# Value products of an RWKV feed-forward as seven half-size products, with weight sums kept in DRAM

## The chip, the cores and the metric

The kernel runs on one core of a Trainium2 chip. A core has a matrix engine (TensorE, in profiles PE, with its weight loads as PEld), a vector engine (VectorE, DVE), an activation engine (ScalarE, ACT), GpSimd (POOL) and SyncE (SP), which here only issues transfers. The metric is device time of one execution in microseconds (us); lower is better.

## What is computed

A local-global attention over 8 batches of 8 heads, 512 local and 32 global positions, head size 64, whose output is the input of a feed-forward in the manner of RWKV. All is float32.

```python
s_ll = np.where(np.abs(pos[:, None] - pos[None, :]) <= 32, scale * q_l @ k_l.T, -1e9)
out_l = softmax([scale * q_l @ k_g.T, s_ll]) @ [v_g, v_l]     # window of 32 to each side, and the global keys
out_g = softmax(scale * q_g @ [k_g, k_l].T) @ [v_g, v_l]
x = concatenate([out_g, out_l])                                # 8 batches, 544 positions, 512 channels
xk = mu_k * x + (1 - mu_k) * x_prev                            # x_prev: the position before
xr = mu_r * x + (1 - mu_r) * x_prev
k = maximum(xk @ w_k, 0)                                       # w_k: 512 x 1024
v = (k * k) @ w_v                                              # w_v: 1024 x 512
out = sigmoid(xr @ w_r) * v                                    # w_r: 512 x 512
```

## The kernel before

**Feed-forward.** Channels lie on the 128 partitions, tokens on the free axis, 256 tokens (`TOK`) to a step: each batch of 512 local tokens is two objects `Tokens` (halves of the batch), and the 8 x 32 global tokens make a seventeenth, at the end. float32 products are made of parts that TensorE takes in one pass (`F32R`): each operand is split into a high part and the rest, and `products` (L381 to 385) issues three matmuls per 128-row chunk, high x high, high x rest, rest x high, all 128x128 by 128x256, into a half of a PSUM bank. The three weights come as 64-bit words; `decode` turns a chunk of 128 x 512 into its two parts with ScalarE, VectorE and GpSimd, paced by `next(decoding)` in the code of the first batch, and the parts stay in SBUF for the whole run.

For each `Tokens`, `mix` makes xk and xr in parts (VectorE L408 and L412, ScalarE L416, GpSimd L417); `keys_and_gate` makes 8 chunks of k in 4 steps of 24 matmuls, each followed by relu on ScalarE (L429), the square on GpSimd (L431) and on ScalarE as high part (L434) and the rest on VectorE (L435), and then the gate in 2 steps of 24 (copy to SBUF L449, sigmoid L451); `values` makes the product with w_v in 4 steps of 24 matmuls, multiplies by the gate (VectorE L463) and stores through SP's queue (L474).

**Attention.** Heads go in units of two, units in pairs, two pairs to a batch. `scores` (32 matmuls of 64x64 tiles, L241), eight masked reductions on VectorE (L246), eight exponentials on ScalarE (L251), the division on GpSimd (L260), `transposes` (L273) and their copies; `scores_global` (L298, reductions L299 and L303); `transposes_global` (L322, L323); `weighted` (matmuls L339 for the windows, L352 for the global queries, L364 for the global keys; copies L370, L372 and L375). Its results xT are the input of `mix` of the same batch.

**Buffers and order.** PSUM has 8 banks: 2 for the feed-forward (tag m), 4 for scores and the global results (tag s), 2 for transposes and `weighted` (tag t). The code emits attention of batch b + 1 and the feed-forward of batch b in turns (`together`), a step at a time; `feed_forward` puts `values` of one `Tokens` behind `mix` of the next. From this program a planner, which simulates the engines when the kernel is built, fixes the order on each engine: it takes the ready instruction that comes earliest in the code, and places the semaphore waits. At run time every engine, and SP's queue of transfers, works strictly in that order. Inputs q and k (L198) and v (L203) of a pair have two buffers each, so the next pair's loads wait until the present pair's matmuls have read theirs. The first batch's attention and keys run beside the decoding of the weights, in an order written out at L572 to L659; batch 7 has no attention beside its feed-forward.

## Time and profile before

| | |
|---|---|
| median of 3 runs | 714.57 us (713.87 to 714.68) |
| profiled execution | 713.56 us, of which 711.8 us span |
| mean granted TensorE clock | 0.978 of full speed |
| matmuls of the feed-forward (L383 to 385) | 4080, of which `values` 1632 |
| transfers | 66.73 MB, mean 94 GB/s |
| stages: first batch's attention, weights | 0 to some 70 us |
| two pairs of heads beside a batch's feed-forward | 79.9 us |
| feed-forward of the last batch and the global tokens alone | 611.5 us to the end |

In the profile's rows an L is a line of the kernel. A group row gives line, engine, operation, output and inputs, shapes and count, then busy time in us, mean ns of one, idle time of the engine before them and what ended it. A window row gives the stretch in us, its length, for each engine the busy time and the count of instructions (PE, PEld, DVE, ACT, POOL, or PE alone), then the granted TensorE clock, the share of the transfer engines' time and GB/s. A wait row gives total us, times, and the longest. A timeline row gives start, length, engine, line, operation and count. Rows of SPq are SP's queue: what a transfer waited for before it was issued.

### The profile page before, as it was taken

To read this page: it belongs to the slowest core of one execution; us is meant where nothing else is said; L and a number is where in the kernel's file an instruction comes from. 1 tells how busy PE (TensorE), PEld (TensorE's weight loads), DVE (VectorE), ACT (ScalarE), POOL (GpSimd) and SP (SyncE) were. 2 spreads that over 40 slices of the span, in tenths; PEclk is the share of its full clock that TensorE was granted. 3 is DMA by queue.
4 is the path that set the end of the run, shared out by engine and by line. 5 is a ranking of instruction groups with operands and counts; after the bars stand their busy time and mean duration, and the time that the engine had idled before them with its cause. 6 is when DMAs were issued, how large, how long until landed. Compare 5 with 4: busy or idle time off the path is not lost.

```text
span 711.8 us, 18514 instructions
## 1 busy us (share of the span) xinstructions
PE 684.2 (96%) x7616; PEld 645.3 (91%) x7616; DVE 360.0 (51%) x1134; ACT 394.8 (55%) x1075; POOL 298.6 (42%) x325
## 2 busy tenths in 40 slices
PE   5789799999999999999999999999999999999997
PEld 3568689989999999999999999899999999999997
DVE  5797976347254362736354363636354352534511
ACT  5877976365565565646565565646565553332420
POOL 6577685136253353424243353424243351323420
PEclk9788889999999999999999999999999999999999
DMA  8735334151423040403222040403222020000000
GB/s 343 279 98 205 128 124 167 39 179 38 158 74 107 16 164 31 164 32 96 98 84 97 17 163 31 164 30 107 88 90 91 16 80 26 17 16 30 2 30 30
DMA packets 21716, 66.73 MB, mean 94 GB/s; under 512 B 2176, under 2 KB 10880, under 8 KB 21632
## 3 DMA queue, kind: packets, MB, share of 16 engines
q1 hardware_dynamic: 21632, 65.55, 25.9%
q8 instruction: 60, 0.98, 0.6%
q14 instruction: 24, 0.20, 0.1%
HBM read 56.63 MB, written 8.91 MB: 92 GB/s over the span
## 4 chain that ended last, share of the span: by engine, by line
PE 77%; DVE 9%; ACT 7%; issue 3%; POOL 2%; DMA 2%; SPq 0%; POOLq 0%; DVEq 0%
PE ps_m L383 21%; PE ps_m L385 20%; PE ps_m L384 20%; PE ps_t L273 4%; PE ps_t L339 4%; PE ps_s L241 3%; ACT Pt L251 3%; DVE xfull L412 2%; PE ps_t L364 2%; DVE Pt L246 2%; POOL k L431 1%; DVE kkl L435 1%; DMA raw_qk<-qk 1%; PE ps_t L322 1%; PE ps_s L352 1%
## 5 line engine op out<-in xcount | busy, mean ns | idle before, releaser
L383 PE MATMUL ps_m<-xkh,wk_h 128*128 128x256 f32 x544 | 157.0, 290 | 2.5 <-ACT gate L446 2.5
L383 PE MATMUL ps_m<-kkh,wv_h 128*128 128x256 f32 x544 | 154.7, 284 | 0.0
L384 PE MATMUL ps_m<-xkl,wk_h 128*128 128x256 f32 x544 | 153.6, 283 | 0.0
L385 PE MATMUL ps_m<-xkh,wk_l 128*128 128x256 f32 x544 | 152.9, 281 | 0.0
L385 PE MATMUL ps_m<-kkh,wv_l 128*128 128x256 f32 x544 | 151.2, 278 | 0.3 <-POOL wv_l L182 0.3
L384 PE MATMUL ps_m<-kkl,wv_h 128*128 128x256 f32 x544 | 151.0, 278 | 0.0
L260 POOL TENSOR_TENSOR Pt<-Pt,ssum 128x512 f32<-128x512 f32 x64 | 67.8, 1060 | 156.0 <-DVE ssum L211 152.6
L251 ACT ACTIVATE Pt<-Pt,m 128x160 f32<-128x160 f32 x256 | 106.5, 417 | 40.6 <-DVE m L246 39.6
L431 POOL TENSOR_TENSOR k<-relu 128x512 f32<-128x512 f32 x68 | 73.4, 1079 | 125.8 <-ACT relu L429 125.8
L429 ACT ACTIVATE relu<-ps_m 128x512 f32<-128x512 f32 x68 | 40.6, 596 | 125.0 <-PE ps_m L385 122.8
L383 PEld LDWEIGHTS ps_m<-xkh,wk_h 128*128 128x128 f32 x544 | 104.0, 192 | 4.5 <-ACT gate L446 2.8
L383 PEld LDWEIGHTS ps_m<-kkh,wv_h 128*128 128x128 f32 x544 | 102.2, 188 | 3.6 <-issue 2.8
L384 PEld LDWEIGHTS ps_m<-xkl,wk_h 128*128 128x128 f32 x544 | 104.9, 193 | 0.0
L385 PEld LDWEIGHTS ps_m<-xkh,wk_l 128*128 128x128 f32 x544 | 104.0, 191 | 0.0
L385 PEld LDWEIGHTS ps_m<-kkh,wv_l 128*128 128x128 f32 x544 | 102.2, 188 | 0.5 <-POOL wv_l L182 0.5
L384 PEld LDWEIGHTS ps_m<-kkl,wv_h 128*128 128x128 f32 x544 | 102.2, 188 | 0.0
L435 DVE TENSOR_TENSOR kkl<-k,kkh 128x512 fp32r<-128x512 f32 x68 | 51.4, 756 | 98.0 <-POOL k L431 96.9
L246 DVE CUSTOM_DVE_ANT_0 Pt<-ps_s,masks 128x160 f32<-128x160 f32 x256 | 66.9, 318 | 45.7 <-PE ps_s L241 45.7
L383 PE MATMUL ps_m<-xrh,wr_h 128*128 128x256 f32 x272 | 79.6, 293 | 0.0
L384 PE MATMUL ps_m<-xrl,wr_h 128*128 128x256 f32 x272 | 76.9, 283 | 0.0
L385 PE MATMUL ps_m<-xrh,wr_l 128*128 128x256 f32 x272 | 76.8, 282 | 0.0
L417 POOL TENSOR_TENSOR xkl<-xfull,xkh 128x512 fp32r<-128x512 f32 x34 | 44.7, 1314 | 74.3 <-ACT xkh L416 74.3
(93 smaller groups left out, 1279.6 us busy)
## 6 DMA issues: line engine op xcount, KB each, us to landing
raw_qk<-qk SPq DMA_DIRECT2D x32, 768.0 KB, 5.7
raw_v<-v SPq DMA_DIRECT2D x32, 640.0 KB, 4.9
out_l<-gate SPq DMA_DIRECT2D x32, 256.0 KB, 2.2
w<-w_k SPq DMA_DIRECT2D x8, 512.0 KB, 9.3
w<-w_v SPq DMA_DIRECT2D x8, 512.0 KB, 3.6
w<-w_r SPq DMA_DIRECT2D x4, 512.0 KB, 3.9
out_g<-gate SPq DMA_DIRECT2D x2, 256.0 KB, 2.1
mu_k_sb<-mu_k SPq DMA_DIRECT2D x1, 2.0 KB, 11.2
```

The costliest lines, as they stand in the source:

```text
L246: nc.vector.tensor_tensor_reduce(out=Pt[:, i], in0=place(e, t, h), in1=masks[:, e, slots[t][1]], op0=ALU.add, op1=ALU.min, scale=-scale, s ...
L251: nc.scalar.activation(Pt[:, i], Pt[:, i], AF.Exp, bias=low_x[:, i:i + 1], scale=-1.0, accum_out=ssum[:, i:i + 1],)
L260: nc.gpsimd.tensor_mul(out, Pt[:, each, at:at + n], rinv.unsqueeze(2).to_broadcast([P, 4, n]))
L273: nc.tensor.transpose(tp[:, i], r.Pt[:, 4 * e + i, SG * e:SG * e + W], ident)
L339: nc.tensor.matmul(op[t][h * D:(h + 1) * D, j, e, a], s.v[:, h, i], r.PT[:, e, 2 * t + h, a * BL:(a + 1) * BL], start=(t, h) not in begun, ...
L383: nc.tensor.matmul(out, w_h[:, i, cols], x_h(i), start=(i == 0), stop=False)
L384: nc.tensor.matmul(out, w_h[:, i, cols], x_l(i), start=False, stop=False)
L385: nc.tensor.matmul(out, w_l[:, i, cols], x_h(i), start=False, stop=(i == n - 1))
L417: nc.gpsimd.tensor_sub(lo[:, both], xf, hi[:, both].bitcast(F32))
L429: nc.scalar.activation(rk, kp, AF.Relu)
L431: nc.gpsimd.tensor_mul(k2, rk, rk)
L435: nc.vector.tensor_sub(kl, k2, kh.bitcast(F32))
```

## The change

**Seven products.** For each batch the product of w_v (512 channels by 1024) with the squared keys (1024 by 512 tokens) is cut in halves in all three directions and made in Winograd's form of Strassen's scheme: seven products of half size on sums and differences, in place of eight. A1 and A2 index the halves of the weights, B of the keys, the second index of B the half of the batch. Sums of the weights, S1 = A21 + A22, S2 = S1 - A11, S3 = A11 - A21, S4 = A12 - S2, are made once; of the keys, T1 = B12 - B11, T2 = B22 - T1, T3 = B22 - B12, T4 = B21 - T2, in each batch. The products are A11 B11, A12 B21, S2 T2 (`values_1`) and S3 T3, S1 T1, A22 T4, S4 B22 (`values_2`), of 4 chunks x 2 x 3 = 24 matmuls each. Two banks X and Y take turns; sums of products stay in a bank or are made on VectorE and ScalarE through three SBUF tiles. The first product's tokens get their channels in two writes, at different times; the gate product is on GpSimd where its input is in SBUF.

**Keys.** The squares stay whole (`k2p`: B11, B21, B12, B22, T2, with T1, T3 and T4 written over B11, B12 and B21) and are split into parts only as operands: 14 tiles of 128x512 a batch, B blocks on ScalarE and VectorE, T blocks on ScalarE and GpSimd. Before it was 8 tiles a batch.

**Weights of the values.** `value_weights` decodes two chunks at a time, makes the sums, splits them, and writes A11 to S4 in parts to a DRAM scratch (8 writes of 1 MB). They are no longer in SBUF; `load_left` reads the left side of each product as two tiles of 512 KB, through 5 buffers, two products ahead, in every batch. Their pools take the place of the first stage's (`stage`, `first_units`, `sums`).

**Order.** `values_1` of the batch before goes ahead of the keys of half 0, `values_2` ahead of those of half 1; in the first batch both halves' keys come first, then both gates, then the products. The global tokens keep four products (`values_of_one`), with their keys between `values_1` and `values_2` of the last batch.

**Attention in one piece.** From batch 2 on the matmuls of a `scores` and of a `weighted` are chained (`Run`): each follows the one before on TensorE with raised priority, and the first has a wait on all the copies that the later ones need: `scores` on the last reads of its banks, `weighted` on the copies of the transposes and on the reduction L303 of the next pair's `scores_global` (`reads["g"]`).

```diff
-    stage = ctx.enter_context(tc.tile_pool(name="stage", bufs=3))
...
-    gatep = ctx.enter_context(tc.tile_pool(name="gatep", bufs=2))
+    gatep = ctx.enter_context(tc.tile_pool(name="gatep", bufs=3))
     tmpp = ctx.enter_context(tc.tile_pool(name="tmpp", bufs=3))
-    mlp1 = ctx.enter_context(tc.tile_pool(name="mlp1", bufs=1))
-    mlp = ctx.enter_context(tc.tile_pool(name="mlp", bufs=2))
+    sump = ctx.enter_context(tc.tile_pool(name="sump", bufs=3))
+    k2p = ctx.enter_context(tc.tile_pool(name="k2p", bufs=1))
+    dramp = ctx.enter_context(tc.tile_pool(name="dramp", bufs=1, space=bass.MemoryType.DRAM))
...
+    stage = place(early_s, "stage", 3, side="right")
+    first_units = place(early_u, "first_units", side="right")
...
+    def split(val, hi, lo, engine=None):
         nc.scalar.copy(hi, val)
-        nc.gpsimd.tensor_sub(lo, val, hi.bitcast(F32))
+        (engine or nc.gpsimd).tensor_sub(lo, val, hi.bitcast(F32))
...
+    LEFT = ("A11", "A21", "A12", "A22", "S1", "S2", "S3", "S4")
+    HC = NF // 2
+    scratch = dramp.tile([P, len(LEFT), HC, 2, TOK], F32, name="scratch")
+    def value_weights():
+        for i in range(HC):
+            A, S = (sums.tile([P, 4, 2, TOK], F32R, tag="x", name=f"left_{x}") for x in "as")
+            s = sums1.tile([P, 4, TOK], F32, tag="s", name="s")
+            a = []
+            for j in range(2):
+                val = decode(staged.pop(0), "s").rearrange("p (j n) -> p j n", j=2)
+                split(val, A[:, 2 * j:2 * j + 2, 0], A[:, 2 * j:2 * j + 2, 1])
+                a.append(val)
+            nc.vector.tensor_add(s[:, 0], a[0][:, 1], a[1][:, 1])
+            nc.vector.tensor_sub(s[:, 2], a[0][:, 0], a[0][:, 1])
+            nc.vector.tensor_sub(s[:, 1], s[:, 0], a[0][:, 0])
+            nc.vector.tensor_sub(s[:, 3], a[1][:, 0], s[:, 1])
+            split(s, S[:, :, 0], S[:, :, 1])
+            for j, part in ((0, A), (4, S)):
+                nc.sync.dma_start(out=scratch[:, j:j + 4, i], in_=part.bitcast(F32))
+            load_chunk()
+            load_chunk()
+            yield
+    V1 = (("A11", "B11"), ("A12", "B21"), ("S2", "T2"))
+    V2 = (("S3", "T3"), ("S1", "T1"), ("A22", "T4"), ("S4", "B22"))
+    to_load = [a for a, _ in V1 + V2] * B + ["A11", "A21", "A12", "A22"]
+    left = []
+    def load_left():
+        if to_load:
+            a = LEFT.index(to_load.pop(0))
+            for i in range(0, HC, 2):
+                part = leftp.tile([P, 2, 2, TOK], F32R, tag="a", name="a")
+                nc.sync.dma_start(out=part.bitcast(F32), in_=scratch[:, a, i:i + 2])
+                left.append(part)
...
+        run = Run(reads["s"] if slots[0][0].b > 1 else None)
...
+    class Run:
+        def __init__(self, copies=None):
+            self.copies, self.last = copies, None
+        def matmul(self, *a, **kw):
+            if self.copies is None:
+                nc.tensor.matmul(*a, **kw)
+                return
+            if self.last is not None:
+                with tc.issue_after(self.last.ins), tc.high_priority():
+                    self.last = nc.tensor.matmul(*a, **kw)
+                return
+            self.last = nc.tensor.matmul(*a, **kw)
+            for c in self.copies:
+                tc.add_manual_dep(
+                    self.last.ins, c.ins.name,
+                    mybir.DependencyInfo(mybir.DependencyClass.Sync, mybir.DependencyReason.DATA),
+                )
...
+        reads["g"] = nc.vector.tensor_tensor_reduce(
...
+    class Keys:
+        def __init__(self, tokens):
+            self.tokens = tokens
+            self.k, self.parts = {}, {}
+        def block(self, name):
+            self.k[name] = k2p.tile([P, HC, TOK], F32, tag=name, name=name)
+            return self.k[name]
+        def keys(self, t):
+            n = self.tokens.index(t) + 1
+            return t.keys([self.block(f"B{i}{n}") for i in (1, 2)])
+        def differences(self):
+            k = self.k
+            k["T1"], k["T3"], k["T4"] = k["B11"], k["B12"], k["B21"]
+            for out, a, b in (("T1", "B12", "B11"), ("T2", "B22", "T1"), ("T3", "B22", "B12"), ("T4", "B21", "T2")):
+                nc.vector.tensor_sub(k[out] if out != "T2" else self.block("T2"), k[a], k[b])
+        def split(self, *names):
+            for b in names:
+                self.parts[b] = []
+                for i in range(0, HC, 2):
+                    h, l = (rightp.tile([P, 2, TOK], F32R, tag=x, name=f"b{x}") for x in "hl")
+                    split(self.k[b][:, i:i + 2], h, l, nc.vector if b[0] == "B" else nc.gpsimd)
+                    self.parts[b].append((h, l))
+        def product(self, out, b, fresh=True):
+            right = self.parts.pop(b)
+            for i in range(HC):
+                a, (b_h, b_l) = left[i // 2], right[i // 2]
                 for j in range(2):
-                    products(vp[:, j], wv_h, wv_l, slice((e0 + j) * P, (e0 + j + 1) * P),
-                             lambda f: self.kk_h[f], lambda f: self.kk_l[f], NF)
-                    if j == 0:
-                        yield
-                o = self.gate[:, e0:e0 + 2]
-                nc.vector.tensor_mul(o, vp, o)
-                self.store(slice(e0, e0 + 2), o)
-                yield
-    FF_STEPS = 10
+                    a_h, a_l = (a[:, i % 2, x, j * P:(j + 1) * P] for x in range(2))
+                    for n, (w, x) in enumerate(((a_h, b_h), (a_h, b_l), (a_l, b_h))):
+                        nc.tensor.matmul(
+                            out[:, j], w, x[:, i % 2], start=fresh and (i, j, n) == (0, 0, 0),
+                            stop=(i, n) == (HC - 1, 2), skip_group_check=True,
+                        )
+            del left[:HC // 2]
+            load_left()
+        def bank(self):
+            return psum("m").rearrange("p (j n) -> p j n", j=2)
+        def sum(self):
+            return sump.tile([P, 2, TOK], F32, tag="sum", name="sum")
+        def values_1(self):
+            t = self.tokens[0]
+            X, Y = self.bank(), self.bank()
+            self.product(X, "B11")
+            c11, self.u2 = self.sum(), self.sum()
+            nc.scalar.copy(c11, X)
+            yield
+            self.product(Y, "B21")
+            nc.vector.tensor_add(c11, Y, c11)
+            t.write(0, c11)
+            yield
+            self.product(X, "T2", fresh=False)
+            nc.scalar.copy(self.u2, X)
+            yield
+            self.split("T3", "T1", "T4")
+        def values_2(self):
+            t0, t1 = self.tokens
+            u2, u3 = self.u2, self.sum()
+            X, Y = self.bank(), self.bank()
+            self.product(X, "T3")
+            nc.vector.tensor_add(X, X, u2)
+            nc.scalar.copy(u3, X)
+            self.split("B22")
+            yield
+            self.product(Y, "T1")
+            nc.vector.tensor_add(u3, Y, u3)
+            t1.write(1, u3)
+            yield
+            self.product(X, "T4", fresh=False)
+            t0.write(1, X)
+            yield
+            self.product(Y, "B22", fresh=False)
+            nc.vector.tensor_add(u2, Y, u2)
+            t1.write(0, u2)
+            yield
...
+        for n, t in enumerate(this.tokens):
             t.mix()
             if before is not None:
-                yield from before.values()
-            yield from t.keys_and_gate()
-            before = t
+                yield from (before.values_1, before.values_2)[n]()
+            if n:
+                this.split("B11", "B21")
+            yield from this.keys(t)
+            if n:
+                this.differences()
+                this.split("T2")
+            yield from t.gates()
...
+                weighted(pair, xTs, PG, copies=A.copies + C.copies + [copy, reads["g"]] if pair[0].b > 1 else None)
...
+        first[1].mix("k")
+        for _ in keys[1]:
             next(decoding)
             yield
-        first[1].mix()
-        for _ in keys[1]:
-            next(decoding, None)
-            yield
-        for t in first:
-            yield from t.values()
-    beside_heads(rest_of_first(), 2 * FF_STEPS - 2)
-    last = None
+        yield from first[0].gates(whole_gate=False)
+        first[1].mix("r")
+        yield from first[1].gates(whole_gate=False)
+        early_u.close()
+        early_s.close()
+        nonlocal leftp, rightp
+        leftp, rightp = place(ctx, "leftp", 5, side="right"), place(ctx, "rightp", 6, side="right")
+        load_left()
+        load_left()
+        last.split("B11", "B21")
+        last.differences()
+        last.split("T2")
+        yield from last.values_1()
+        yield from last.values_2()
...
+    def end():
+        yield from steps[0]
+        t.mix()
+        yield from before.values_1()
+        yield from final.keys(t)
+        yield from t.gates()
+        yield from before.values_2()
+        final.split("B11", "B21")
+        yield from final.values_of_one()
```

130 lines of the change are left out of this document (74 added, 56 removed).

## Prediction, made before the changed kernel was timed

> **What bounds the kernel now.** I read the page first (busy shares, slices, the chain by engine), then windows of TensorE, then the waits. From the page:
>
> ```profile
> span 711.8 us, 18514 instructions
> PE 684.2 (96%) x7616; PEld 645.3 (91%) x7616; DVE 360.0 (51%) x1134; ACT 394.8 (55%) x1075; POOL 298.6 (42%) x325
> ...
> PE   5789799999999999999999999999999999999997
> ...
> PEclk9788889999999999999999999999999999999999
> DMA  8735334151423040403222040403222020000000
> ...
> PE 77%; DVE 9%; ACT 7%; issue 3%; POOL 2%; DMA 2%; SPq 0%; POOLq 0%; DVEq 0%
> ```
>
> TensorE is the bound from the sixth slice (about 89 us) on, at a full granted clock; no other engine is near it. But busy PE only says that some matmul is under way (a line's mean of 280 ns is latency, not cost), so a saved matmul must be priced by its pace. Windows that hold known blocks of matmuls give that; their counts in brackets include neighbours that reach in, so I count from the code:
>
> ```profile
> 97.00:707.80 610.80, 606.54 (x6851) 582.74 (x6849) 282.68 (x900) 320.21 (x858) 233.50 (x241) 1.00 0.22 77
> 614.46:625.34 10.88, 10.88 (x98) 1.00 0.07 26
> 509.99:512.93 2.94, 2.94 (x29) 1.00 0.00 0
> 513.28:516.11 2.83, 2.83 (x28) 1.00 0.26 93
> ```
>
> The first row is everything from 97 us to the last matmul: TensorE stands for 4.26 us of 610.8. The second is `values` of one token half beside no attention: 96 matmuls in 10.88 us, 113.3 ns each, 2.72 us for a block of 24. The other two are single blocks of 24 between pieces of attention: 2.94 and 2.83 us. The extra 0.1 to 0.2 us is the change to and from attention's small matmuls.
>
> The waits of TensorE and two windows, the first a `weighted` of the middle batches, the second the last one:
>
> ```profile
> PE ps_s L241 <- DMA raw_qk<-qk: 6.3, 3, 5.1
> PE ps_t L339 <- DVE mg L303: 3.9, 10, 0.4
> ...
> 491.35:496.32 4.97, 4.58 (x121) 4.28 (x120) 4.97 (x11) 2.29 (x9) 3.08 (x4) 1.00 0.47 192
> 607.22:611.49 4.27, 4.27 (x121) 4.08 (x120) 3.20 (x8) 0.62 (x1) 1.40 (x1) 1.00 0.02 4
> ...
> 492.57 0.58 DVE L303 CUSTOM_DVE_ANT_0 Pg<-ps_t,low,mg 128x384 f32<-128x384 f32 x1
> ```
>
> Ten times `weighted` is cut and stands 0.4 us for VectorE's L303, which still reads the banks it needs; the uncut one takes 0.70 us less for the same matmuls.
>
> **The change part by part.**
>
> *Products.* Per batch, `values` had 2 halves x 4 x 8 x 3 = 192 matmuls; seven products of 4 x 2 x 3 = 24 are 168. The operand shapes stay. So 24 go in each of 8 batches; the global tokens keep their 96. At 113.3 ns that is 8 x 2.72 = **-21.8 us**; at 2.94 a block, -23.5. I take the lower, since the number of changes to attention barely falls. From 97 us on TensorE has no slack, so what is removed there shows in full if the operands are on time.
>
> *Engines behind the products, per batch.* The rows:
>
> ```profile
> L435 DVE TENSOR_TENSOR kkl<-k,kkh 128x512 fp32r<-128x512 f32 x68 | 51.4, 756 | 98.0 <-POOL k L431 96.9 <-PE ps_m L384 1.1
> L434 ACT ACTIVATE kkh<-relu 128x512 fp32r<-128x512 f32 x68 | 43.3, 636 | 1.6
> L463 DVE TENSOR_TENSOR gate<-ps_m,gate 128x512 f32<-128x512 f32 x34 | 23.5, 691 | 94.1 <-PE ps_m L385 94.1
> L417 POOL TENSOR_TENSOR xkl<-xfull,xkh 128x512 fp32r<-128x512 f32 x34 | 44.7, 1314 | 74.3 <-ACT xkh L416 74.3
> L260 POOL TENSOR_TENSOR Pt<-Pt,ssum 128x512 f32<-128x512 f32 x64 | 67.8, 1060 | 156.0 <-DVE ssum L211 152.6 <-PE ps_m L385 3.5
> ...
> 509.99:549.95 39.96, 39.57 (x466) 37.83 (x462) 19.10 (x67) 23.25 (x64) 15.51 (x17) 1.00 0.25 87
> 549.95:589.90 39.95, 39.56 (x445) 38.17 (x442) 19.18 (x66) 21.93 (x63) 16.04 (x17) 1.00 0.13 48
> ```
>
> The last two windows are one batch: 79.9 us with DVE 38.3, ACT 45.2, POOL 31.6. VectorE loses 8 kkl and 4 gate products (8.8 us) and gains 6 splits of B11, B21, B22, 4 differences of twice that width and 5 operations on the products: 6 x 0.756 + 8 x 0.756 + 5 x 0.691 = 14.0; it ends at 43.5. ScalarE loses 8 squares (5.1) and gains 14 casts and 3 copies of like size, 17 x 0.636 = 10.8: 50.9. POOL gains 8 splits of T blocks and 3 gate products, 8 x 1.314 + 3 x 1.060 = 13.7: 45.3. A batch now lasts about 77 us, so all three stay under 66%: hidden. If that cover failed, the price would be the chain behind a single product, about 1.5 us (0.691 plus 0.636 and the hops); it lies beside the next product's 2.72 us, since X and Y alternate. T2, the last operand to be made, has the gate blocks (5.8 us) and two products ahead of it. I put the leftover stalls, from a burst of score reductions ahead of such an operation, at **+2** for the run, between 0 and 12 (1.5 us in each of 8 batches).
>
> *Streamed left halves.* Each batch reads 7 x 1 MB, as 14 loads of 512 KB.
>
> ```profile
> raw_qk<-qk SPq DMA_DIRECT2D x32, 768.0 KB, 5.7
> ...
> w<-w_v SPq DMA_DIRECT2D x8, 512.0 KB, 3.6
> ...
> 114.46:117.00 2.54, 2.54 (x24) 2.54 (x23) 2.54 (x4) 0.73 (x3) 2.54 (x4) 1.00 1.01 419
> ...
> SPq L474 <- DVE gate L463: 210.5, 21, 28.2
> ...
> 488.38 0.83 SPq L198 DMA_DIRECT2D raw_qk<-qk  x2
> ...
> 508.81 1.25 PE ps_s L241 x32
> ```
>
> The 7.3 MB add 95 GB/s to the 48 to 87 of the batch windows; the queue moved 419 at full share. One product's 1.05 MB takes 2.5 us at that, a product 2.72: even back to back the stream keeps up, and two and a half products lie ready at the start of each burst. A half freed at a product's middle lands 3.6 us later, 4.96 us after that product began, and is needed at 2 x 2.72 + 1.36 = 6.8. Cost nothing, as long as SP issues each load when its buffer is free. The next pair's `raw_qk` loads have slack: issued at 488.4 behind the scores of one pair, they are read from 508.8 on and land in 5.7. Bound: one whole landing, 3.6 us, per burst (below, third rival).
>
> *Attention in one piece.* From batch 2 on the score and `weighted` matmuls follow each other, and the first waits for all the copies, for `weighted` also for L303 of the next pair (`reads["g"]`). By the last row above L303 ended at 493.2, 1.8 us after `weighted` began at 491.35. The planner must put other matmuls there, and the next gate block (2.9 us) is at hand. Best: 10 x 0.70 = -7.0. Worst: TensorE stands the whole 1.8 us, and everything behind it on its queue with it, so 10 x (1.8 - 0.7) = +11. I take **-4**, nearest the row of the uncut piece, with some cuts moved into a gate block. The score runs wait for the reductions of the scores before, several steps back: nothing.
>
> *Start.* The sums of the value weights, their way through DRAM and the new order fall into the stretch where TensorE isn't yet full:
>
> ```profile
> 60.00:80.00 20.00, 19.95 (x217) 17.46 (x215) 18.11 (x45) 16.80 (x41) 11.49 (x11) 1.00 0.51 174
> 80.00:97.00 17.00, 12.32 (x76) 10.88 (x74) 13.70 (x35) 14.95 (x38) 15.09 (x16) 0.70 0.27 83
> 97.00:115.80 18.80, 18.80 (x263) 17.35 (x262) 14.85 (x41) 15.93 (x42) 11.99 (x10) 1.00 0.58 186
> 115.80:149.00 33.20, 32.88 (x401) 31.17 (x401) 13.24 (x56) 13.99 (x49) 11.63 (x15) 1.00 0.27 99
> ...
> L182 POOL TENSOR_TENSOR wv_l<-w,wv_h 128x512 fp32r<-128x512 f32 x8 | 10.8, 1353 | 2.7 <-ACT wv_h L181 2.7
> ...
> L408 DVE TENSOR_TENSOR diff<-xT 128x256 f32<-128x256 f32 x64 | 32.3, 543 | 14.8 <-ACT xT L375 14.3
> ...
> 111.20 0.69 DVE L178 SCALAR_TENSOR_TENSOR w<-w,ps_s 128x512 int32<-128x512 int32 x1
> ...
> 115.78 0.28 PE L383 MATMUL ps_m<-kkh,wv_h 128*128 128x256 f32 x1
> ```
>
> Batch 0's `values` began at 115.8. In the 55.8 us before it DVE was busy 46.7, ACT 47.7, POOL 38.6. Added on VectorE: 16 sums and 4 doubled `diff` at 0.543 (10.9), T1 and T2 as four of 0.756 (3.0), B11 and B21 as four (3.0), less 8 kkl (6.0): +10.9, more than the 9.1 that were free. POOL: 8 half-size pieces of the sums' splits at 1.353 and two of T2 at 1.314: +13.4 against 17.2 free. And nothing may start until the last A11 and A12 have been split (1.35), written as 1 MB (about 5, from 3.6 for half of it) and read again (3.6): 10 us behind the last decode, which ended on VectorE at 111.9 (L178). That is 121.9, 6 us later. Of the window that follows, 33.2 less 21.8 of products = 11.4 us is attention, part of which can go ahead. I take **+4**, between -3 (the mix of half 1 is split, so its keys need less ahead of them; TensorE idled 4.7 us in 80 to 97) and +18 (the whole 10 us plus the overfull engines, nothing brought forward).
>
> Rows on one operation at two prices, same line, two instructions each:
>
> ```profile
> 488.87 0.88 DVE L412 SCALAR_TENSOR_TENSOR xfull<-diff,mu_k_sb,xT 128x256 f32<-128x256 f32 x2
> ...
> 490.92 1.64 DVE L412 SCALAR_TENSOR_TENSOR xfull<-diff,mu_r_sb,xT 128x256 f32<-128x256 f32 x2
> ```
>
> So VectorE operations nearly double at times. The Trainium skill, in "SBUF — State Buffer", section "Who interferes with whom", says why that may be: VectorE, with two inputs in SBUF, and GpSimd take turns on one pair of ports, and the later one waits for the whole instruction. By that rule the 13.4 us added on POOL at the start would come on top of VectorE's and push `values` back by up to as much; it is the mechanism of the first rival.
>
> **Sum.** 713.56 us is the profiled execution's time (1.8 us around its span of 711.8): -21.8 - 4 + 4 + 2 = 693.8. The median of the runs shown is 1.0 us higher: **694.8**.
>
> **The rivals.**
> *Start late, still faster.* VectorE and POOL, both overfull, hold each other up, and batch 0's products begin 20 us late with little to fill in: 14 us above the forecast, 709. For it: 60 to 80 us has VectorE at 18.1 of 20, and the doubled operation above. Against: attention can fill in, and wv's decode is now due ahead of the gates. 0.16.
> *Better than forecast.* Start at -3, pieces at -7, no stalls: 683. For it: the almost unbroken row from 97 us. 0.10.
> *Loads late, slower.* SP is one queue. A store waits there for its gate product, up to 28.2 us in the row above; a left load behind it isn't issued though its buffer is free, and each of two bursts a batch stands a whole landing: 16 x 3.6 = 58, so 752; half of them, 723. It decides from 25 / 16 = 1.6 us a burst on: then nothing is left. Against: SP's order follows the planned time of each wait, and its waits today cost TensorE almost nothing. 0.11, told as 735.
> *Waits in every batch.* `weighted` pays its +11 and products stall by the bound of 12: the gain is gone, about 714. 0.05.
>
> **How the numbers follow.** Forecast 0.58, its own range 686 to 702. Range 683 to 712: it takes in the forecast, the late start and half of the better case. A measurement of this kernel can tell about 0.2% (1.4 us) from no change. Faster: 0.58 + 0.16 + 0.10 = 0.84; the same 0.04; slower 0.12.
>
> **What would show it.** Right: two pairs of heads last 75.5 to 77.5 us instead of 79.9; TensorE's waits name no left tile; `values` of the last batch keep 2.7 us a product; the first product of batch 0 begins at 118 to 126. Wrong: TensorE waiting for a DMA into `a`, for L303 ahead of `weighted`, or for ScalarE's and VectorE's reads of X and Y; DVE and POOL full up to 130 us.

## The result and the profile after

| | before | after |
|---|---|---|
| median of the runs | 714.22 us (713.76 to 714.68, 4 runs) | 747.67 us (743.83 to 748.07, 4 runs) |
| ratio, with its 95% interval | | 1.0456 (1.0421 to 1.0492) |
| span of the profiled execution | 711.8 us | 746.2 us |
| first product of batch 0 begins at | 115.8 us | 137.8 us |

The changed kernel is 4.6% slower, where 694.8 us was forecast with a range of 683 to 712. TensorE does 192 matmuls less and its span is 34.4 us longer. The page of the changed kernel, with the lines that answer to those shown of the kernel before:

```profile
span 746.2 us, 18626 instructions
...
PE 684.0 (92%) x7424; PEld 639.5 (86%) x7424; DVE 429.3 (58%) x1178; ACT 427.9 (57%) x1151; POOL 428.7 (57%) x417
...
PE   5788985889999999899989999899989999898996
...
PEclk9779998799999999999999999999999999999999
DMA  9636589695215456363826184536536181452546
...
PE 64%; DVE 13%; ACT 5%; issue 2%; DMA 2%; POOL 1%; POOLq 0%; ACTq 0%; DVEq 0%; SPq 0%
```

TensorE's busy time is what it was (684.0 against 684.2 us) although it has less to do, and from the sixth slice on its line of slices has 8s and one 5 (112 to 131 us) among the 9s, where it had 9s alone. On the chain that ended last VectorE rose from 9% to 13%. So the loss has two sides: TensorE stands more, and its matmuls take longer. The windows of TensorE up to the first product show the first place (columns as in the windows of before; the last pair of numbers is DMA share and GB/s):

```profile
80.00:97.00 17.00, 15.38 (x145) 14.43 (x143) 13.41 (x31) 10.23 (x26) 15.22 (x12) 1.00 0.72 233
97.00:115.80 18.80, 18.00 (x184) 15.66 (x184) 15.60 (x33) 15.60 (x30) 14.13 (x12) 0.91 0.80 288
115.80:137.80 22.00, 12.66 (x143) 9.73 (x141) 13.84 (x66) 18.71 (x60) 10.91 (x11) 0.77 0.85 292
```

In the last 22 us, in which the kernel before was already at its products, TensorE is busy 12.66, at a granted clock of 0.77. The waits of TensorE name the second place (what waited, what released it: us in total, times, longest):

```profile
PE ps_m L575 <- DVE gate L527: 15.0, 6, 3.1
...
PE ps_t L353 <- ACT xT L457: 6.0, 2, 5.6
PE ps_m L575 <- ACT sum L610: 3.0, 2, 2.9
PE ps_m L575 <- ACT sum L593: 2.0, 1, 2.0
...
PE ps_m L575 <- DMA a<-scratch: 2.0, 3, 1.6
```

L575 is the matmul of a product, L527 the copy of a gate block out of PSUM: six times a product waits for it. The transposes of the global scores (L402) of the same pair in two batches that follow each other, and the window from the one to the other, give the length of a batch:

```profile
417.87 0.60 PE L402 MATMUL ps_t<-ident,Pg 128*128 128x128 f32 x4
...
497.28 0.49 PE L402 MATMUL ps_t<-ident,Pg 128*128 128x128 f32 x3
```

```profile
417.87:497.28 79.41, 76.50 (x901) 73.00 (x899) 43.85 (x135) 49.62 (x137) 46.24 (x46) 1.00 0.52 180
```

79.4 us against 79.9 before and some 77 forecast, with VectorE, ScalarE and POOL busy for 43.9, 49.6 and 46.2 us (forecast: 43.5, 50.9 and 45.3). The sums of the engines' work were right; that it would be hidden was not.

### The profile page after: what moved, and what is told of

Its sections match the earlier page's. It is cut to its first block, busy times and chain, and to the rows that moved or that the text cites. A ratio compares the mean times of both kernels' runs of the same rounds, so it can differ in the third digit from the quotient of the medians.

```text
span 746.2 us, 18626 instructions
## 1 busy us (share of the span) xinstructions
PE 684.0 (92%) x7424; PEld 639.5 (86%) x7424; DVE 429.3 (58%) x1178; ACT 427.9 (57%) x1151; POOL 428.7 (57%) x417
## 4 chain that ended last, share of the span: by engine, by line
PE 64%; DVE 13%; ACT 5%; issue 2%; DMA 2%; POOL 1%; POOLq 0%; ACTq 0%; DVEq 0%; SPq 0%
PE ps_m L575 21%; PE ps_m L464 9%; PE ps_m L465 9%; PE ps_m L466 9%; DVE xfull L496 5%; PE ps_t L332 4%; PE ps_s L332 4%; PE ps_t L353 2%; ACT Pt L307 2%; DVE B L558 2%; DVE Pt L301 1%; DVE T L558 1%; DMA a<-scratch 1%; PE ps_s L334 1%; PE ps_t L378 1%
## 5 line engine op out<-in xcount | busy, mean ns | idle before, releaser
L575 PE MATMUL ps_m<-bh,a 128*128 128x256 f32 x960 | 189.7, 292 | 23.4 <-DVE gate L527 15.0
L575 PEld LDWEIGHTS ps_m<-bh,a 128*128 128x128 f32 x960 | 156.5, 196 | 27.5 <-DVE gate L527 16.2
L575 PE MATMUL ps_m<-bl,a 128*128 128x256 f32 x480 | 139.0, 290 | 1.2 <-DVE bl L191 1.2
L316 POOL TENSOR_TENSOR Pt<-Pt,ssum 128x512 f32<-128x512 f32 x64 | 69.4, 1084 | 81.0 <-DVE ssum L265 75.0
L512 POOL TENSOR_TENSOR B<-relu 128x512 f32<-128x512 f32 x68 | 72.3, 1065 | 71.0 <-ACT relu L511 69.2
L575 PEld LDWEIGHTS ps_m<-bl,a 128*128 128x128 f32 x480 | 93.9, 196 | 2.1 <-DVE bl L191 1.4
L191 POOL TENSOR_TENSOR bl<-B,bh 128x512 fp32r<-128x512 f32 x48 | 63.1, 1341 | 18.0 <-ACT bh L190 18.0
L190 ACT CAST bh<-B 128x512 fp32r<-128x512 f32 x100 | 60.8, 622 | 19.5 <-PE ps_m L575 15.8
L496 DVE SCALAR_TENSOR_TENSOR xfull<-diff,mu_r_sb,xT 128x256 f32<-128x256 f32 x64 | 58.6, 944 | 15.3 <-POOL B L512 12.5
```

Source lines behind the costliest of these rows:

```text
L190: nc.scalar.copy(hi, val)
L191: (engine or nc.gpsimd).tensor_sub(lo, val, hi.bitcast(F32))
L316: nc.gpsimd.tensor_mul(out, Pt[:, each, at:at + n], rinv.unsqueeze(2).to_broadcast([P, 4, n]))
L496: nc.vector.scalar_tensor_tensor(self.shape(xf[:, j]), self.shape(diff[:, j]), mu[:, c0 + j:c0 + j + 1], self.prev(c0 + j), op0=ALU.mult, ...
L512: nc.gpsimd.tensor_mul(k2[f0 // HC][:, f0 % HC:f0 % HC + 2], rk, rk)
L575: nc.tensor.matmul(out[:, j], w, x[:, i % 2], start=fresh and (i, j, n) == (0, 0, 0), stop=(i, n) == (HC - 1, 2), skip_group_check=True,)
```

## Experiments

Ratios are to the kernel before on the same chip; the interval is 95%. Line numbers are those of the changed kernel, a little lower in runs that take lines out.

### The wait for the gate copy

What stands ahead of the copy in VectorE's queue, at one of the six waits (timelines of VectorE, POOL and TensorE in the changed kernel; start, length, instruction, idle time before it):

```profile
302.49 2.12 DVE L558 TENSOR_TENSOR T<-B,B 128x1024 f32<-128x1024 f32 x1
304.54 1.21 DVE L558 TENSOR_TENSOR B<-B,B 128x1024 f32<-128x1024 f32 x1
305.67 2.97 DVE L496 SCALAR_TENSOR_TENSOR xfull<-diff,mu_r_sb,xT 128x256 f32<-128x256 f32 x2
308.57 0.31 DVE L301 CUSTOM_DVE_ANT_0 Pt<-ps_s,masks 128x160 f32<-128x160 f32 x1
...
309.82 1.21 DVE L558 TENSOR_TENSOR B<-B,T 128x1024 f32<-128x1024 f32 x1
310.96 0.16 DVE L265 RECIPROCAL ssum<-ssum 128x4 f32<-128x4 f32 x1
311.05 0.65 DVE L527 COPY gate<-ps_m 128x512 f32<-128x512 f32 x1
```

```profile
305.34 3.02 POOL L191 TENSOR_TENSOR bl<-T,bh 128x512 fp32r<-128x512 f32 x2 [1.81 <-ACT bh L190]
```

```profile
308.58 0.28 PE L466 MATMUL ps_m<-xrh,wr_l 128*128 128x256 f32 x1
311.75 0.39 PE L575 MATMUL ps_m<-bh,a 128*128 128x256 f32 x1 [2.90 <-DVE gate L527]
```

The feed-forward has two PSUM banks. The next product needs the bank of the first gate block, and that comes free only when VectorE, in the order of its queue, has made the differences T2, T3 and T4, two `xfull` and a burst of reductions. **Gate copy on ScalarE:**

```diff
-                nc.vector.tensor_copy(self.gate[:, e0:e0 + 2], rp)
+                nc.scalar.copy(self.gate[:, e0:e0 + 2], rp)
```

> The changed kernel with the copy of the gate product out of PSUM (L527) on ScalarE in place of VectorE, nothing else. Theory: TensorE's waits of 15.0 us in 6 places for L527 come from VectorE's queue, in which the copy stands behind differences and an xfull doubled by GpSimd; they go, and with them the stretches of half clock that follow some of them: 728 to 733. Rival: VectorE's sums of products, L596 and the like, are as late, and the wait only changes its name: 742 to 748.

Measured: 732.28 us (731.75 to 735.27), ratio 1.0278 (1.0254 to 1.0301). The wait is down to a third:

```profile
PE ps_m L575 <- ACT gate L527: 5.3, 5, 1.1
```

By the ratios that is 1.8% or 12.7 us of 713, by the medians 15.4. The wait itself gave 15.0 - 5.3 = 9.7. The rest fits the stretches at half clock that follow some stalls (last section): behind 150 us the changed kernel has four of them, at 1.7 us each, and this run has none. This cause is shown.

In the timeline above the two `xfull` take 1.5 us each beside POOL's split of T2; two took 0.88 together in the row shown of the kernel before. The Trainium skill, in "SBUF — State Buffer", section "Who interferes with whom", has VectorE with two inputs in SBUF and GpSimd take turns on a shared port, and the trace agrees: counted over all `xfull` of the trace, the 81 that had no POOL instruction beside them took about 0.48 us, and the 34 that took 1.2 us and more all stood beside one; the other 21, beside one in part or in whole, took 0.47 to 1.04. Is POOL's split the cause of the long queue? **T2's split on VectorE:**

```diff
-                    split(self.k[b][:, i:i + 2], h, l, nc.vector if b[0] == "B" else nc.gpsimd)
+                    split(self.k[b][:, i:i + 2], h, l, nc.vector if b[0] == "B" or b == "T2" else nc.gpsimd)
```

> The changed kernel with the rest of T2's split on VectorE instead of POOL; the gate copy stays on VectorE. In the changed kernel xfull took 0.48 us in all 81 cases with no POOL instruction beside it and 1.5 us in 33 cases beside one. Theory: POOL's split of T2 doubles or trebles the operations that stand ahead of the gate copy in VectorE's queue; without it TensorE's wait for the gate copy falls from 15.0 us to 6 to 11 and the time by 4 to 9 us, to 739 to 744. Rival: the two splits now stand in VectorE's queue themselves (1.4 us) ahead of the copy and make up for it; 745 to 751.

Measured: 745.33 us (743.63 to 751.97), ratio 1.0467 (1.0415 to 1.0519): no gain. The same place in VectorE's timeline:

```profile
302.16 2.12 DVE L558 TENSOR_TENSOR T<-B,B 128x1024 f32<-128x1024 f32 x1
...
305.33 0.87 DVE L496 SCALAR_TENSOR_TENSOR xfull<-diff,mu_r_sb,xT 128x256 f32<-128x256 f32 x2
...
308.60 2.10 DVE L191 TENSOR_TENSOR bl<-T,bh 128x512 fp32r<-128x512 f32 x2
310.63 0.68 DVE L527 COPY gate<-ps_m 128x512 f32<-128x512 f32 x1
```

The `xfull` are back at 0.87 for two, so the shared port did cost 2.1 us there; but the split now stands in the queue itself for 2.1 us, and the copy comes 8.47 us behind the difference T2 where it came 8.56 behind it. The rival held: at this place the length of VectorE's queue counts, not who made it long.

### The start

The chain in the changed kernel: the last chunk of w_v is loaded, decoded, summed and split, written to DRAM, and read again. Its DMA issues on SP, and the first product:

```profile
108.06 0.34 SPq L164 DMA_DIRECT2D w<-w_v  x1
...
117.32 0.36 SPq L226 DMA_DIRECT2D scratch<-left_a  x1
117.77 1.65 SPq L252 DMA_DIRECT2D raw_qk<-qk  x1
119.51 1.43 SPq L257 DMA_DIRECT2D raw_v<-v  x2
121.16 0.60 SPq L226 DMA_DIRECT2D scratch<-left_s  x1
131.17 2.64 SPq L241 DMA_DIRECT2D a<-scratch  x5
```

```profile
137.81 0.39 PE L575 MATMUL ps_m<-bh,a 128*128 128x256 f32 x1 [1.28 <-ACT bh L190]
```

Two readings offer themselves: the trip of S through DRAM (from 121.2 to 131.2 the first load stands behind the last write), or the sums' work on the engines.

**No sums** (`value_weights` without the four sums and their split; A is written a second time in place of S):

```diff
-            nc.vector.tensor_add(s[:, 0], a[0][:, 1], a[1][:, 1])
...
-            split(s, S[:, :, 0], S[:, :, 1])
-            for j, part in ((0, A), (4, S)):
+            for j, part in ((0, A), (4, A)):
```

> The changed kernel, whose S1 to S4 are left out: A11 to A22 are written to DRAM a second time in their place, so the sums of the weights and their split go (4 small VectorE operations, a cast and a GpSimd subtraction of 1024 columns, four times), and the transfers stay. The first product of the first batch began at 137.8 us, of the kernel before at 115.8. Theory: the way through DRAM is most of the 22 us (a write that landed 9.3 us after its issue and a read of 6.6), so it begins at 130 to 134. Rival: the engines' work for the sums is most of it: 116 to 124.

One run: 733.88 us, first product at 128.7: between the two theories, so both seemed to have a part. Four ways to shorten or cover the trip followed.

**Products of batch 0 one stage later** (`rest_of_first` ends with the split of T2; batch 1's feed-forward takes the products of batch 0 as later batches do):

```diff
         last.split("T2")
-        yield from last.values_1()
-        yield from last.values_2()
+        yield
...
-    before = None
+    before = last
```

> The changed kernel with the products of batch 0 moved one stage later: the first stage ends with the split of T2, and batch 0's seven products stand in the feed-forward stage of batch 1, as every later batch's do. Theory: the 22.2 us by which the first product came later (137.8 against 115.8 us) is TensorE standing while the last sums go through DRAM and back; one stage later there is other work, so most of it goes: 726 to 732 us. Rival: in the new place nothing else is ready for TensorE either (the planner put little beside the wait), and the idle time only moves: 743 to 750 us.

Measured: 753.21 us (748.75 to 761.22), ratio 1.0542 (1.0513 to 1.0571). The first product began at 148.2, behind a cast of B11 on ScalarE. The idle time only moved.

**Two DRAM tensors** (with the gate copy on ScalarE):

```diff
-    scratch = dramp.tile([P, len(LEFT), HC, 2, TOK], F32, name="scratch")
+    scratch = [dramp.tile([P, 4, HC, 2, TOK], F32, name=f"scratch_{x}") for x in "as"]
```

> The changed kernel with the gate copy on ScalarE, and the halves A and the sums S kept in two DRAM tensors instead of one. In the run with the gate copy alone the first loads of A11 were issued at 130.9 us, when the last write of S (issued at 121.1) had landed, although they read only A, whose last write was issued at 117.3. Theory: the one tensor makes them wait; with two they go out about 8 us earlier, the first product comes at 129 to 132 us instead of 137.8, and the time is 724 to 728 us instead of 732.3. Rival: the wait is for the space of the sums or for the same full DMA queues, or ScalarE's queue is late next; the first product stays at 135 to 138 and the time at 730 to 733.

Measured: 732.35 us (731.93 to 733.12), ratio 1.0264 (1.0248 to 1.0279), first product at 137.9: nothing. The first load takes the SBUF space in which the last S had been made (both lie at byte 208864 of a partition), so it waits for the write of S whatever the tensor in DRAM.

The run called five edits below, two DRAM tensors among them, was the base of two more. **One more chunk buffer:**

```diff
-    stage = place(early_s, "stage", 3, side="right")
+    stage = place(early_s, "stage", 4, side="right")
...
-    for _ in range(3):
+    for _ in range(4):
         load_chunk()
```

> As the run with five edits, with four buffers instead of three for the weight chunks on their way in. The loads of chunks waited 18 us in the changed kernel for VectorE's sums to set a buffer free. Theory: that wait paces the start; one more buffer lets the decode end 3 to 6 us earlier and the time falls by as much. Rival: VectorE's and POOL's own work paces it; within 1.5 us of the run with five edits.

Measured: 726.23 us (724.63 to 727.09), ratio 1.0177 (1.0154 to 1.0200), against 724.46 without: nothing. **Other places for the buffers**:

```diff
+    for _ in range(2):
+        nc.gpsimd.memset(sums.tile([P, 4, 2, TOK], F32, tag="x", name="turn")[:, 0, 0, 0:1], 0.0)
...
-        leftp, rightp = place(ctx, "leftp", 5, side="right"), place(ctx, "rightp", 6, side="right")
+        rightp = place(ctx, "rightp", 6, side="right")
+        place(ctx, "apart", side="right").tile([P, 16], F32, tag="apart", name="apart")
+        leftp = place(ctx, "leftp", 5, side="right")
```

> As the run with five edits, with the buffers of the sums and of the left and right halves moved about: the first load of A11 went into the space that the last sums S had held, so it waited until the write of S to DRAM had landed (131.7 us in the run with two DRAM tensors), and the next loads stood behind it on SP though their space was free. Now the last S lies where only a half of A12 and later ones go. Theory: the first loads go out when the last A has been written (it landed at 122.8), the first product begins at 126 to 131 us and the time is 716 to 720 us against 724.5. Rival: ScalarE's cast of B11, which came at 137.2 behind the exponentials, or the prefetch of the next heads that shares the DMA engines, is late next; first product at 134 to 138, time 722 to 726.

Measured: 731.58 us (730.35 to 739.13), ratio 1.0287 (1.0228 to 1.0345). The first load did go out ahead of the landing of S, at 127.7, but the new turn of the sums' buffers put the last write of A at 123.3 instead of 117.4, and the first product at 141.9. As a test of the trip it is inconclusive.

The next pair of runs parts the two readings, both with the gate copy on ScalarE. **No write of S**, then **neither sums nor S** (the edit shown is the first; the second also leaves out the four sums and their split). In both the products with S read A in its place:

```diff
-            for j, part in ((0, A), (4, S)):
-                nc.sync.dma_start(out=scratch[:, j:j + 4, i], in_=part.bitcast(F32))
+            nc.sync.dma_start(out=scratch[:, 0:4, i], in_=A.bitcast(F32))
...
-                nc.sync.dma_start(out=part.bitcast(F32), in_=scratch[:, a, i:i + 2])
+                nc.sync.dma_start(out=part.bitcast(F32), in_=scratch[:, a % 4, i:i + 2])
```

> The changed kernel with the gate copy on ScalarE; the sums S are computed and split as before but not written to DRAM, and the products with S read A from DRAM instead. So the engines' work of the start stays, and the first loads wait for the last write of A alone. Theory of the trip: most of the start's loss is the wait for the write of S, 9.3 us of it: first product at 127 to 131 us instead of 137.8, time 723 to 727 instead of 732.3. Theory of the engines: VectorE, POOL and ScalarE with the sums' 9 us pace the start, and the operand B11 comes behind them whatever the loads do: first product at 134 to 138, time 729 to 733.

> As the run without the write of S, and the sums and their splits are left out too. What this gains over it is the sums' work on the engines, what is still missing against the kernel before is the trip of A through DRAM and the work around it. Theory of the trip: first product at 120 to 125, 4 to 7 us less than the run without the write. Theory of the engines: first product at 120 to 125 too, but 9 to 14 us less than the run without the write, since that one gained nothing.

Measured: 731.33 us (729.05 to 734.49), ratio 1.0243 (1.0207 to 1.0278), without the write; 714.46 us (712.43 to 718.59), ratio 1.0022 (1.0001 to 1.0042), without sums and S. The first products, of the one and of the other:

```profile
135.68 0.56 PE L574 MATMUL ps_m<-bh,a 128*128 128x256 f32 x1
```

```profile
120.28 0.39 PE L568 MATMUL ps_m<-bh,a 128*128 128x256 f32 x1 [1.15 <-DMA a<-scratch]
```

Against the run with the gate copy alone the trip of S is worth 1.0 us by the medians and 2.5 by the ratios, whose intervals overlap; the sums' work is worth 16.9 us by the medians and 15.8 by the ratios, and 15.4 us of the first product's delay. The windows of the run without sums show where the time comes from:

```profile
80.00:97.00 17.00, 17.00 (x161) 16.29 (x160) 10.00 (x31) 11.82 (x32) 10.03 (x10) 1.00 0.69 229
...
115.80:137.80 22.00, 18.10 (x176) 16.70 (x176) 18.53 (x51) 16.39 (x48) 13.70 (x12) 0.92 0.81 311
```

Between 80 and 97 us VectorE has 3.4 us less to do than in the changed kernel and POOL 5.2, and TensorE stands no more there. At the end the first product waits for a load, not for ScalarE's cast. The engines' theory held as to the price. The path is shown in part only. The last decode on VectorE (L184) begins at 113.5 without the write of S and at 107.7 without the sums: 5.7 us of the 15.4. Without the write the first load was issued at 120.6 instead of 130.9 and the cast of B11 began at 125.6 instead of 137.1, and yet the first product came no earlier than 135.7: TensorE's queue has it behind transposes of attention, and these waited 4.2 us for ScalarE's xT and 3.8 for VectorE's copy. So the trip was hidden behind other queues. Where the sums are gone it does show: the first product came at 128.7 in the run without sums that kept the second write, and at 120.3 without both (the two runs differ in the gate copy too).

### The pace of the matmuls

Windows over blocks of 48 matmuls with no attention beside them (the counts include neighbours): gates of the kernel before; gates, then products of the changed kernel.

```profile
636.22:641.97 5.75, 5.75 (x50) 5.75 (x49) 4.49 (x8) 1.85 (x3) 2.45 (x2) 1.00 0.00 0
```

```profile
652.91:658.66 5.75, 5.75 (x50) 5.75 (x49) 3.97 (x8) 1.11 (x2) 2.29 (x2) 1.00 0.00 0
658.67:664.40 5.73, 5.73 (x50) 5.69 (x48) 4.35 (x7) 4.69 (x8) 3.39 (x3) 1.00 0.50 142
```

5.75 us by 48 are 120 ns: the new products run at the pace of the gates, not at the 113.3 ns of the old products. The two operands of the slow kinds lie, in the program as built, at SBUF addresses that are equal modulo 128 bytes (products: 184288 and 208864, both 96; gates: 167456 and 106016, both 32), those of the fast kinds 64 apart. **64 bytes between left and right halves:**

```diff
-        leftp, rightp = place(ctx, "leftp", 5, side="right"), place(ctx, "rightp", 6, side="right")
+        leftp = place(ctx, "leftp", 5, side="right")
+        place(ctx, "apart", side="right").tile([P, 16], F32, tag="apart", name="apart")
+        rightp = place(ctx, "rightp", 6, side="right")
```

> The changed kernel with the right sides of the products moved by 64 bytes in SBUF against the left sides, nothing else. In the traces a matmul follows the last after 113.3 ns in keys of both kernels and in the values of before, and after 120.0 ns in the gates of both and in the new products. In the first group the addresses of the two operands differ by 64 modulo 128, in the second they are equal modulo 128. Theory: that is the cause; the products go at 113.3 ns, 1440 x 6.7 = 9.6 us less: about 738. Rival: the new order, where every third matmul changes between two halves of a bank, is the cause: products stay at 120.0 ns and the time at 747.

Measured: 743.50 us (741.73 to 744.32), ratio 1.0418 (1.0400 to 1.0436). 48 products:

```profile
626.27:631.71 5.44, 5.44 (x50) 5.40 (x48) 3.91 (x8) 2.61 (x4) 3.03 (x3) 1.00 0.47 133
```

113.3 ns: a shift of 64 bytes alone restores the pace. The time fell by 4.2 us by the medians (2.7 by the ratios, whose intervals overlap), where 9.6 were expected. Over the whole trace the products that follow each other directly came down from 119.5 to 114.1 ns, which is 7.8 us for 1440, while the keys rose from 114.9 to 115.6; where the rest went isn't shown. **The same shift ahead of the gate weights, in the kernel before:**

```diff
+    ctx.enter_context(tc.tile_pool(name="shift", bufs=1, reuse_waits="tile")).tile([P, 16], F32, name="shift")
     gatew = ctx.enter_context(tc.tile_pool(name="gatew", bufs=1, reuse_waits="tile"))
```

> The kernel before, with 64 bytes per partition left empty ahead of the gate weights, so that their addresses and those of xr differ by 64 modulo 128 bytes; no instruction is added. Theory: the 120.0 ns of a gate matmul against 113.3 ns of the others comes from the two operands' addresses; 816 gate matmuls at 6.7 ns are 5.5 us, so 706.5 to 709 us against 713 of the kernel before, and gate matmuls at 113.3 ns. Rival: the pace belongs to something else in these matmuls (their weights, their output banks); then 712 to 714 us and 120.0 ns stay.

Measured: 713.19 us (712.35 to 713.70), ratio 1.0001 (0.9992 to 1.0009). The gates did speed up:

```profile
636.08:641.51 5.43, 5.43 (x50) 5.43 (x49) 4.17 (x8) 1.85 (x3) 2.23 (x2) 1.00 0.00 0
```

So the theory of the pace held and that of its price fell: the time is the same. Beside attention the old products run slower in this run than in the kernel before (116.5 ns from start to start on average over all products of the trace that follow each other directly, instead of 115.2), since more of them have the third pace of the last section; why, stays open.

### Attention in one piece

The kernel before with `Run` and its waits alone:

```diff
+        run = Run(reads["s"] if slots[0][0].b > 1 else None)
...
-                        nc.tensor.matmul(
+                        run.matmul(
```

> The kernel before with attention in one piece alone; products, keys and weights as before. Theory: the cuts in weighted go and the wait costs little, since the planner puts a gate block there; attention's share of a batch fell from 21.9 to 20.4 us in the changed kernel, so this gives 6 to 9 us: 705 to 708. Rival, the bound of the prediction: TensorE stands for L303 of the next pair each time, +11 us: about 725.

Measured: 711.76 us (710.62 to 713.33), ratio 0.9985 (0.9975 to 0.9994): a gain of 1.1 us. TensorE's waits in it, from 150 us on:

```profile
PE ps_t L299 <- issue: 3.5, 5, 0.7
PE ps_m L412 <- POOL xkl L445: 0.4, 1, 0.4
```

`weighted` waits no more for VectorE, as forecast, but at five runs a short time goes by before their first matmul, and the cuts that left attention went into the blocks of products: TensorE turns from the feed-forward to attention 118 times instead of 117, out of gates 15 times instead of 26 and out of products 54 instead of 42. About a quarter of the forecast gain is there.

### The edits together

**Four edits** are the gate copy, both shifts and the later products; in **values first** w_v is also decoded ahead of w_r; **five edits**, as the run is called on record, are the gate copy, both shifts and the two DRAM tensors, with the products of batch 0 where the change has them. The edit of values first:

```diff
-    for src, cols in ((w_k, DF), (w_r, NC * P), (w_v, NC * P)):
+    for src, cols in ((w_k, DF), (w_v, NC * P), (w_r, NC * P)):
...
-    decoding = chain(weights(range(NK, NK + NC), wr_h, wr_l), value_weights())
+    decoding = chain(value_weights(), weights(range(NK + NF, NK + NF + NC), wr_h, wr_l))
```

> The changed kernel with four edits: gate copy on ScalarE, 64 bytes between left and right halves, 64 bytes ahead of the gate weights, batch 0's products one stage later. Theory: the four losses lie at different places and add up: 747.7 - 15.4 - 4.2 - 5.5 - 18 = 704.6, so 701 to 709 us, faster than the kernel before. Rival: they are largely the same stalls seen from several sides; then 714 to 722 us, no faster than the kernel before.

> As the run with four edits, and the value weights are loaded, decoded, summed and written to DRAM ahead of the gate weights instead of behind them. If the trip through DRAM still holds TensorE up at the start, some 4 to 10 us less than the run with four edits; if the move to the next stage already covers it, the same within 1.5 us.

> As that run, with 64 bytes between left and right halves and 64 bytes ahead of the gate weights; batch 0's products stay where the change has them. Theory: the paces of products and gates are 113 to 114 ns and add to what the run with two DRAM tensors gains: 8 to 10 us below it, 715 to 719 us. Rival: the shorter matmuls only lengthen waits for operands, as in the kernel before, where the faster gates gave nothing: within 3 us of that run.

Measured: 728.99 us (728.05 to 729.16), ratio 1.0219 (1.0201 to 1.0236), with four edits; 732.33 us (731.51 to 732.52), ratio 1.0268 (1.0252 to 1.0283), with the values first, whose first product came at 154.2, later than in any other run and against both expectations (why stays open); 724.46 us (723.22 to 725.78), ratio 1.0152 (1.0134 to 1.0171), with five. The last is 7.9 us below the run with the gate copy and two tensors alone: more than the two shifts gave one by one (2.7 to 4.2, and nothing), and about half of the 9.6 + 5.5 that were worked out for them. A batch of it, between its global transposes at 404.62 and 481.14:

```profile
404.62:481.14 76.52, 75.15 (x900) 71.66 (x899) 41.33 (x131) 51.63 (x141) 45.52 (x46) 1.00 0.51 187
```

76.5 us, where the prediction gave 75.5 to 77.5 (77.6 with the gate copy alone). What is left of the loss, 724.46 less 713.58 of the kernel before on that chip, lies outside these batches. By the stages of the table at the end of the next section, the start is 12.5 us longer than in the kernel before and the end, where products follow each other with no attention beside them, 14.0; the middle is 17.0 shorter. The end also has 48 matmuls more than before, since a batch's products now come later.

No version with the seven products beat the kernel before. Attention in one piece without them gained 1.1 us, less than the 1.4 us that the prediction took a measurement to tell.

## Why the prediction was wrong

- **Products, -21.8.** The number of matmuls was right. The step that failed is "At 113.3 ns": the pace was taken from the old products, and the new ones ran at 120.0 ns because of where their operands lie. 1440 matmuls at 6.7 ns are 9.6 us. The rows of the gates, at 120 ns in the kernel before, would have shown that this pace isn't the same for all. Beside attention 113.3 ns was too low for the old products too: the block of 2.94 us, whose length the prediction put down to the change to attention, ran inside at 117.7 ns (starts from 510.22 to 512.81, 22 steps).
- **"So all three stay under 66%: hidden", +2.** The largest failed step of the middle part. The shares came out as forecast, yet the wait for the gate copy alone cost 13 to 15 us, over the upper bound of 12. The price of a failed cover was worked out for the chain behind a product; what was late was a *gate* block's copy, which the change had not touched, behind VectorE operations that the change put ahead of it. A share says how much an engine has to do, not how long the one instruction that holds a bank stands in its queue.
- **Start, +4.** The first product came 22.0 us later, not 6. The step that failed is "10 us behind the last decode, which ended on VectorE at 111.9 (L178). That is 121.9": it adds the trip to a decode that stays where it was, and to the split of A alone. The last decode ended at 115.2, POOL's split of the last sums at 121.1, the first load was issued at 131.2. With the trip of A alone and no sums the first product came at 120.3, near that 121.9, so the trip of A was well priced; the sums' work, 16.9 us in the runs, was not. The prediction had seen VectorE overfull (10.9 us added, 9.1 free) and still took +4 out of its range of -3 to +18. The price stood in the rival *Start late, still faster* (20 us late, 14 us dearer, chance 0.16); that VectorE and POOL hold each other up by their port, as the rival has it, was not tested at the start.
- **Attention in one piece, -4.** Direction right, size 1.1 us in the kernel before. The wait for L303 went as forecast; the cuts moved into the blocks of products instead of vanishing.
- **Streaming, 0.** About right: TensorE waited 2.0 us in all for left halves. The rival *Loads late, slower* fell, and with it the only reason given for a clearly slower kernel.
- **Half clock after stalls.** The sum has no term for it, and it was put at nothing without a reason. The mean granted clock fell from 0.978 to 0.963: 2.2% of 711.8 us and 3.7% of 746.2 are 15.7 and 27.6 us of clock not granted, 11.9 us more (an estimate of its price).
- **Sum of it.** The forecast missed by 52.9 us. Runs that take out one thing each explain 30 to 39 of them, measured less forecast: the start 16.9 - 4 = 13, the gate copy 13 to 15 - 2 = 11 to 13, the pace 3 to 10 (2.7 to 4.2 in the run with 64 bytes between the halves, 9.6 worked out), attention 4 - 1.1 = 3. The profiles account for the whole. TensorE's idle time, its span less its busy time, rose by 34.6 us, where the last three terms of the forecast (-4 + 4 + 2) allowed for 2. Its busy time fell by 0.2 instead of 21.8, since the pace (9.6) and the half clock (11.9) took the saving back. 32.6 + 9.6 + 11.9 = 54.1, and the profiled executions miss by 34.4 + 19.8 = 54.2. Which stall makes which part of the idle time is shown for the gate copy and for the sums of the start, and argued for the rest.

TensorE's idle time by stage, from the windows of the two profiles. The first border is the sixth global transposes, those of batch 2's second pair, the next the same four batches later, then the last matmul of attention:

| | before: length, idle | after: length, idle |
|---|---|---|
| start | 203.0, 19.9 us | 220.6, 36.4 us |
| four batches | 319.4, 3.2 us | 316.2, 11.5 us |
| rest of attention | 89.2, 0.8 us | 89.9, 2.9 us |
| end, no attention | 100.2, 3.7 us | 119.5, 11.4 us |

About half of the new idle time lies in the start. In the middle two stages the gate copy accounts for 8.7 + 2.9 us of waits, in the end for 3.4, beside ScalarE's sums (2.2) and loads (2.0).

## What to carry to other kernels

That an engine is half idle does not make work added to it free: look in its queue for the instruction that frees a PSUM bank or feeds TensorE, and count what will stand ahead of it. Price saved matmuls by the pace of the new ones, and look at where their operands will lie. In a start where the engines are nearly full, price the operations added to them before the transfers: here the sums were worth 16.9 us and the write of S behind them 1.0 to 2.5.

## What the runs showed of the hardware

**Operand addresses.** Matmuls of the same shape follow each other at 113.3 or 120.0 ns, depending on whether the two operands' SBUF addresses are 64 apart or equal modulo 128 bytes; moving one of them by 64 bytes changed it, for products and for gates. A third pace appears with no address changed. Two blocks of 96 key matmuls of the run with five edits:

```profile
620.24:631.53 11.29, 11.29 (x98) 11.29 (x97) 1.50 (x4) 2.90 (x5) 8.56 (x8) 1.00 0.34 114
648.38:659.27 10.89, 10.89 (x98) 10.89 (x97) 3.38 (x7) 1.80 (x3) 4.51 (x4) 1.00 0.67 212
```

117.6 and 113.4 ns, both at a granted clock of 1.00. What sets it stays open.

**Half clock after a stall.** In the changed kernel a product began after a wait of 2.03 us, and TensorE then had half its clock for 3.4 us:

```profile
637.54 0.39 PE L575 MATMUL ps_m<-bh,a 128*128 128x256 f32 x1 [2.03 <-ACT sum L593]
```

```profile
637.91:641.32 3.41, 3.41 (x19) 3.41 (x18) 0.30 (x1) 1.75 (x4) 3.41 (x4) 0.50 0.46 173
```

So a stall of 2 us can cost 1.7 us more. Its length alone does not decide: of the five waits of 2.9 to 3.1 us for the gate copy two were followed by such a stretch. In this trace the stretches behind 300 us begin at 392.16, 552.58 and 637.92, which is 47 and 25 times 3.413 us apart. Windows on that grid (length, TensorE busy, count, clock, DMA share, GB/s), the first two around a stall with a slow stretch behind it, the others around one without:

```profile
549.17:552.58 3.41, 1.16 (x9) 1.00 0.00 0
552.58:555.99 3.41, 3.41 (x25) 0.50 0.40 107
...
685.70:689.12 3.42, 1.69 (x15) 1.00 0.00 0
689.12:692.53 3.41, 2.08 (x17) 1.00 0.00 0
```

The stall of 2.89 us from 548.52 lies mostly in one window, the one of 3.06 us from 687.39 is split between two. TensorE was busy for 1.00, 1.16 and 1.38 us in the windows ahead of the three slow stretches, and for 1.69 us and more on both sides of a border in the three waits without one. So where a stall lies on the grid decided here. The Trainium skill, in "TensorE: Matmul & The Clock Gate", section "Part 1: The HAM clock gate (the "warmup" mystery)", gives half rate after an idle window of about 3.4 us and full rate after a busy one of that length. The length of the slow stretch agrees; the stall before it was shorter than the page's idle window.
